# A linear-attention block with a one-token gated FFN beside it: dummy matmuls around the second tile's transposes, and a later place for two matmul batches and the down rows

## The chip, the cores and the metric

The kernel runs on one core of one Trainium2 chip. The metric is the device time of one execution in microseconds (us). The profiler also gives a span, from the first to the last instruction; of the same execution the time is about 1.7 us longer than the span. Lower is better.

## The reference, cut to what matters

Two blocks read the same `x` (2048 tokens of 1024) and are mixed by a sigmoid gate:

```python
def _A_ref(x, wqkv, wo):                    # linear attention, 32 heads of 32
    q, k, v = split(x @ wqkv)
    phi = lambda t: jnp.where(t > 0, t + 1, jnp.exp(t)) + 1e-6
    pq, pk = phi(q), phi(k)
    kv = einsum("bhsd,bhse->bhde", pk, v);  z = pk.sum(tokens)
    return (pq @ kv / (pq @ z + 1e-6)) @ wo
def _B_ref(x, w_r, w_gate, w_up, w_down):   # ONE token, the one with the largest x @ w_r
    y = (silu(x_sel @ w_gate) * (x_sel @ w_up)) @ w_down      # F = 3584
    return x with sigmoid(r_sel) * y added to that token's row
g = sigmoid((x * gate_w).sum(-1))
return g * a + (1 - g) * b
```

Block A is 16 tiles of 128 tokens times large matrices and fills TensorE. Block B is a single row times three 7 MB matrices: little arithmetic, much weight traffic. The kernel hides B under A.

## The kernel before: the parts that matter

A dummy is a matmul whose result nobody uses; it only keeps TensorE busy. `N_WARM` dummies and three short ones already stand at the start. The schedule of block B is set by tables that say after which unit of tile `t` a piece goes:

```python
N_WARM = 6
GU_AFTER = {(7, "end"): 4, (8, "end"): 4, (10, 3): 8, (12, 1): 8}   # batches of gate/up matmuls
FLUSH_AFTER = {(9, 2), (13, 0)}                                     # hps: turn h, so the down rows can begin
DOWN_STEPS = {10: (1, 1, 1, 1, 1, 1), 11: (1, 1, 1, 1, 1), 12: (1, 0, 1, 1, 1),
              13: (1, 1, 1, 1, 1), 14: (1, 1, 1, 1, 1), 15: (1, 1, 1)}
FFN_DEPTH = 9                                                       # weight buffers
```

The product with `w_down` isn't done on TensorE. VectorE does it in 28 rows, each a 128 x 1024 multiply-add into one accumulator, two rows to a weight tile:

```python
def compute(wt, kk, i2=i2, k0=k0, dk=dk):                 # one down row
    w, h1 = wt[:, 1024 * kk : 1024 * kk + 1024], hcol[:, ...]
    if i2 == 0 and kk == 0:
        dve.tensor_scalar(yacc, w, h1, None, op0=ALU.mult)
    else:
        dve.scalar_tensor_tensor(yacc, w, h1, yacc, op0=ALU.mult, op1=ALU.add)
```

(The accumulator `yacc` shares its memory with the gate sums, so the profile calls it `gacc`.) The same engine takes TensorE's results of the main stream out of PSUM, the memory that TensorE writes to. I call that an eviction: one of 128 x 512 for each key unit (`pk`) and each query unit (`pq_all`); value units are copied out by ScalarE. Key, value and query units share four PSUM buffers (`ps_work`, `bufs=4`).

Weight tiles of B are loaded in the order of `ffn_pieces`, and a load can go only when one of the nine buffers is free:

```python
yield from islice(g0, 6)          # gate tiles that VectorE sums (gacc)
...
for n in (2, 4):                  # 2 down tiles, 8 gate tiles, 4 down tiles, 8 up tiles, 8 down tiles
    yield from islice(dn, n)
    yield from islice(gu, 8)
yield from dn
yield from wo_pieces()
```

The main loop, cut:

```python
for t in range(4, NT):
    for nb in range(4):
        unit_KV(t, nb)                            # 8 matmuls of 512 columns; nb 0,1 key, 2,3 value
        if nb == 1 and t > 4 and t % 4 == 0:
            for t0 in range(t - 4, t):
                unit_KVACC(t0)                    # the kv block
        ffn_step(GU_AFTER.get((t, nb), 0))
        if (t, nb) in FLUSH_AFTER:
            ffn_flush()
        ...
        down_step(steps[nb])
    for i in range(Q_PER_T[t]):
        unit_Q(*q_units.popleft())
        ...
    ffn_step(GU_AFTER.get((t, "end"), 0))
    if t == 8:
        gate_reduce()                             # fp32 sums over partitions (gps), then silu, then h
```

After the loop, `down_finish` sums the 28 rows' accumulator over partitions (`yps`).

## Time and profile before

| before | |
|---|---|
| time, median of the first three runs | 251.35 us (250.92 to 251.53) |
| span of the profiled execution | 251.4 us |
| TensorE busy | 97% |
| VectorE busy | 65% |
| rise of the TensorE clock in that execution | 10.05 us |

Read it as a kernel that TensorE bounds almost everywhere. Time can only be gained where TensorE's stream has a hole or runs at half clock. The lines that carry this are in the prediction below.

### The profile page before, as it was taken

The numbers are of one execution on the slowest core, as the hardware profiler recorded it, in microseconds if no ns is written. First come the engines' busy times: TensorE is split into PE (matmuls) and PEld (weight loads), VectorE is DVE, ScalarE is ACT, GpSimd is POOL, SyncE is SP. The second block draws the span as 40 slices with busy tenths as digits, with TensorE's granted clock in tenths as the row PEclk, the third lists the DMA queues.
The fourth block names the chain that finished last, engine by engine and source line by source line (L and its number), as shares of the span: only waits on it lengthen the run. The fifth ranks groups of instructions, "written<-read, shape, count | busy, mean of one in ns | idle before, by whom it ended". The sixth has DMA issues, their size and how long they took to land.

```text
span 251.4 us, 4171 instructions
## 1 busy us (share of the span) xinstructions
PE 244.6 (97%) x1576; PEld 112.0 (45%) x1602; DVE 163.3 (65%) x257; ACT 125.7 (50%) x200; POOL 51.8 (21%) x102
## 2 busy tenths in 40 slices
PE   8999999999999999999999999999999999999994
PEld 3444445444444534444544444444444444444442
DVE  0036005244999469699699993585888999953442
ACT  2068334455455355545535644568888633333210
POOL 5000002010000100000033000210666689950000
PEclk9999999999999999999999999999999999999999
DMA  6999990008999992489699996130000564454122
GB/s 191 308 344 215 258 341 18 0 5 269 356 348 287 331 288 68 146 297 328 215 310 314 429 349 146 52 132 7 4 0 0 158 220 146 152 183 139 71 83 83
DMA packets 47242, 47.73 MB, mean 190 GB/s; under 512 B 18732, under 2 KB 35380, under 8 KB 47160
## 3 DMA queue, kind: packets, MB, share of 16 engines
q1 hardware_dynamic: 46552, 46.29, 60.2%
q0 software_dynamic: 640, 1.19, 1.6%
q8 instruction: 12, 0.20, 0.3%
q14 instruction: 6, 0.05, 0.1%
q10 hardware_dynamic: 32, 0.00, 0.0%
HBM read 39.34 MB, written 8.40 MB: 190 GB/s over the span
## 4 chain that ended last, share of the span: by engine, by line
PE 95%; DMA 2%; issue 1%; SPq 0%; DVE 0%; DVEq 0%
PE ps L80 87%; PE first L80 3%; DMA xnat<-in_A_x_dram 2%; PE kvacc L80 2%; PE dps L80 1%; PE rps L80 1%; PE pm L80 1%; PE pst L80 0%; PE gps L80 0%; SPq L80 0%; DVE ot L80 0%; PE yps L80 0%; PE xs_ps L80 0%; DVEq L747 0%; PE pt L80 0%
## 5 line engine op out<-in xcount | busy, mean ns | idle before, releaser
L80 PE MATMUL ps<-wkv,xT 128*128 128x512 bf16 x468 | 105.6, 379 | 0.6
L80 PEld LDWEIGHTS <-xT 128*128 128x128 bf16 x512 | 49.9, 99 | 60.9 <-issue 3.0
L80 PE MATMUL ps<-xT,wq 128*128 128x512 bf16 x248 | 57.5, 379 | 0.7 <-issue 0.5
L80 PE MATMUL ps<-m_sb,pq_all 128*128 128x512 bf16 (+2 forms) x259 | 55.3, 372 | 0.3
L80 ACT ACTIVATE u<-ps 128x512 f32<-128x512 f32 x60 | 35.8, 597 | 36.8 <-PE ps L80 36.1
L80 ACT ACTIVATE e<-u 128x512 f32<-128x512 f32 x64 | 40.3, 630 | 2.0
L650 POOL TENSOR_TENSOR pq_all<-pq_all,rb 128x512 bf16<-128x512 bf16 x32 | 36.6, 1172 | 14.4 <-DVE rb L80 14.0
L80 PEld LDWEIGHTS <-pq_all 128*128 128x128 bf16 x264 | 25.5, 98 | 30.2 <-issue 0.4
L80 PEld LDWEIGHTS <-wq 128*128 128x128 bf16 x256 | 24.3, 98 | 30.2 <-issue 2.1
L80 DVE SCALAR_TENSOR_TENSOR pq_all<-ps,e 128x512 bf16<-128x512 f32 x32 | 21.9, 686 | 23.8 <-ACT e L80 23.7
L80 DVE SCALAR_TENSOR_TENSOR gacc<-wt,hcol,gacc 128x1024 f32<-128x1024 bf16 x27 | 34.6, 1282 | 3.8 <-DMA wt<-in_B_w_down_dram 3.3
L80 ACT CAST vt<-ps 128x512 bf16<-128x512 f32 x32 | 18.8, 587 | 31.6 <-PE ps L80 31.6
L80 DVE SCALAR_TENSOR_TENSOR ot<-ps,gate,xg 128x512 bf16<-128x512 f32 (+2 forms) x33 | 23.8, 733 | 15.0 <-PE ps L80 14.2
L80 ACT ACTIVATE xg<-xt,omg 128x1024 f32<-128x1024 bf16 x16 | 18.1, 1145 | 25.9 <-DVE ot L80 25.9
L80 DVE SCALAR_TENSOR_TENSOR pk<-ps,e 128x512 bf16<-128x512 f32 x28 | 19.1, 686 | 7.5 <-ACT e L80 7.5
L209 POOL MEMSET vt<- 128x16 bf16 x16 | 2.4, 199 | 103.2 <-PE kvacc L80 102.6
L80 DVE STREAM_SHUFFLE rb<-rdp 128x512 f32<-128x512 f32 x32 | 22.8, 746 | 0.0
L80 DVE SCALAR_TENSOR_TENSOR gacc<-wt,xs_f,gacc 128x1024 f32<-128x1024 bf16 x14 | 17.4, 1279 | 0.5 <-DMA wt<-in_B_w_gate_dram 0.5
L80 PE MATMUL first<-wkv,xT 128*128 128x512 bf16 x31 | 8.9, 443 | 0.1
L80 DVE SCALAR_TENSOR_TENSOR pk<-first,e 128x512 bf16<-128x512 f32 x4 | 2.8, 692 | 9.3 <-ACT e L80 9.3
L80 DVE CAST r_bf<-rps 128x512 bf16<-128x512 f32 x1 | 0.7, 693 | 12.5 <-PE rps L80 12.5
L80 DVE RECIPROCAL rd<-dn 128x512 f32<-128x512 f32 x2 | 6.7, 3338 | 0.0
(104 smaller groups left out, 89.3 us busy)
## 6 DMA issues: line engine op xcount, KB each, us to landing
wt<-in_B_w_down_dram SPq DMA_DIRECT2D x14, 512.0 KB, 5.5
wt<-in_B_w_gate_dram SPq DMA_DIRECT2D x8, 512.0 KB, 7.3
wt<-in_B_w_up_dram SPq DMA_DIRECT2D x8, 512.0 KB, 8.6
xt<-xp SPq DMA_DIRECT2D x16, 256.0 KB, 3.0
out_dram<-ot SPq DMA_DIRECT2D x15, 256.0 KB, 2.0
wt<-in_B_w_gate_dram SPq DMA_DIRECT2D x8, 384.0 KB, 6.9
wt<-in_B_w_up_dram SPq DMA_DIRECT2D x8, 384.0 KB, 7.6
wkv<-in_A_wqkv_dram SPq DMA_DIRECT2D x8, 256.0 KB, 5.2
```

Source lines behind the costliest of these rows:

```text
L80: inst = fn(*a, **k)
L209: nc.gpsimd.memset(vt_t[t][:, :, :, 64:65], 1.0)
L650: nc.gpsimd.tensor_tensor(sl, sl, rb[:], op=ALU.mult)
```

## The change

The intent has two parts. At the start, short dummy matmuls are to keep TensorE busy around the second tile's transposes, so that its clock comes up early. In the middle, the first batch of up matmuls goes right behind the kv block, which saves a switch between kinds of matmul. The last of those batches goes, with the fp32 gate sums, a unit later, and everything behind them moves along: `hps` and the down rows.

```diff
-GU_AFTER = {(7, "end"): 4, (8, "end"): 4, (10, 3): 8, (12, 1): 8}
-FLUSH_AFTER = {(9, 2), (13, 0)}
+GU_AFTER = {(8, 1): 4, (9, 1): 4, (10, 3): 8, (12, 1): 8}
+FLUSH_AFTER = {(10, 1), (13, 0)}
-DOWN_STEPS = {10: (1, 1, 1, 1, 1, 1), 11: (1, 1, 1, 1, 1), 12: (1, 0, 1, 1, 1), 13: (1, 1, 1, 1, 1), 14: (1, 1, 1, 1, 1), 15: (1, 1, 1)}
+DOWN_STEPS = {10: (0, 1, 1, 1, 1, 1), 11: (1, 1, 1, 1, 1), 12: (0, 0, 1, 1, 1), 13: (1, 1, 1, 1, 1), 14: (1, 1, 1, 1, 2), 15: (1, 1, 1, 1)}
@@ start
-    wps = ps_ffn.tile([P, 16], BF, tag="f")
-    pe.transpose(wps[:], wrg_rows[:], ident[0:16, 0:16])
-    dve.tensor_copy(wrg_pad[:, :, 0:2], wps[:].rearrange(...))
+    pe.matmul(warm_ps[:, 0:16], lhsT=wrg_rows[:], rhs=ident[0:16, 0:16], start=True, stop=True)
+    dve.tensor_copy(wrg_pad[:, :, 0:2], warm_ps[:, 0:16].rearrange(...))
+    warm(4, 128, 128)
     unit_T(1)
+    warm(2, 128, 128)
@@ ffn_pieces
-        for n in (2, 4):
+        for n in (1, 4):
@@ main loop
+            if (t, nb) == (9, 1):
+                gate_reduce()
...
-        if t == 8:
-            gate_reduce()
```

(`warm` also gets an argument for the columns it writes; that is cut here.)

More of the change, by code (lines that the diff above doesn't have):

```diff
@@ L245, with warm @@
     warm_x = nc.const_aps.tensor(1.0, (P, 512), BF)
-    def warm(n, w=512):
+    def warm(n, w=512, o=0):
         for _ in range(n):
-            pe.matmul(warm_ps[:, 0:w], lhsT=warm_w, rhs=warm_x[:, 0:w], start=True, stop=True)
+            pe.matmul(warm_ps[:, o : o + w], lhsT=warm_w, rhs=warm_x[:, 0:w], start=True, stop=True)
     warm(N_WARM)
@@ L263 @@
     first_mm(0, 0, 1)
-    wps = ps_ffn.tile([P, 16], BF, tag="f")
-    pe.transpose(wps[:], wrg_rows[:], ident[0:16, 0:16])
-    dve.tensor_copy(wrg_pad[:, :, 0:2], wps[:].rearrange("p (w c) -> p c w", w=2))
+    pe.matmul(warm_ps[:, 0:16], lhsT=wrg_rows[:], rhs=ident[0:16, 0:16], start=True, stop=True)
+    dve.tensor_copy(wrg_pad[:, :, 0:2], warm_ps[:, 0:16].rearrange("p (w c) -> p c w", w=2))
+    warm(4, 128, 128)
     unit_T(1)
+    warm(2, 128, 128)
     for c in range(1, KC):
```

## The prediction

> **What bounds the kernel now.** I read the page's first part and its chain of waits first, to see which engine sets the end:
>
> ```profile
> span 251.4 us, 4171 instructions
> PE 244.6 (97%) x1576; PEld 112.0 (45%) x1602; DVE 163.3 (65%) x257; ACT 125.7 (50%) x200; POOL 51.8 (21%) x102
> ...
> PE 95%; DMA 2%; issue 1%; SPq 0%; DVE 0%; DVEq 0%
> ```
>
> TensorE (PE) is 97% busy and is 95% of the chain that ends last. VectorE (DVE) at 65% is the next. So a change can pay only by taking time out of the PE stream: a wait in it, a slow clock under it, or a price for switching between kinds of matmul. I looked for each in turn.
>
> The chain in order of time has one real wait, at the start (columns: start us, us, what):
>
> ```profile
> 1.91 4.73 DMA xnat<-in_A_x_dram
> 6.64 0.04 issue
> 6.68 1.03 PE pst L80 x8
> 7.72 5.75 PE first L80 x21
> ```
>
> The second 128-row tile of x lands at 6.64 us, its eight transposes (pst) follow, then the first matmuls. After that it is PE all the way to the last output. Next, the timeline of weight loads (PEld) in the opening stretch; each load precedes one matmul, so the distance between starts is the matmul step:
>
> ```profile
> 8.37 0.15 PEld L80 LDWEIGHTS <-xT 128*128 128x128 bf16 x1 [0.28 <-issue]
> 8.79 0.15 PEld L80 LDWEIGHTS <-xT 128*128 128x128 bf16 x1 [0.28 <-issue]
> 9.22 0.15 PEld L80 LDWEIGHTS <-xT 128*128 128x128 bf16 x1 [0.28 <-issue]
> 9.64 0.15 PEld L80 LDWEIGHTS <-xT 128*128 128x128 bf16 x1 [0.28 <-issue]
> 10.06 7.87 PEld L80 LDWEIGHTS <-xT 128*128 128x128 bf16 x37 [0.27 <-issue]
> ```
>
> Until 10.06 a 512-wide matmul takes a step of 0.427 us, afterwards 7.87/37 = 0.213 (0.216 from the starts of single matmuls). The trace's clock record has the rise at 10.05 us; the PEclk row prints 9 from the start and doesn't show it. Six useful matmuls run at half speed, from 7.51 to 10.05.
>
> In the PE timeline of the same stretch the hole before the second tile's transposes is visible:
>
> ```profile
> 4.94 1.06 PE L80 MATMUL first<-wkv,xT 128*128 128x512 bf16 x2
> 5.94 0.19 PE L80 MATMUL wps<-ident,wrg_rows 16*128 16x16 bf16 x1
> 6.68 1.03 PE L80 MATMUL pst<-ident,xnat 128*128 128x128 bf16 x8 [0.56 <-DMA xnat<-in_A_x_dram]
> ```
>
> For the middle part I read the PE and DVE timelines around the up batches (ps<-wt,xs_pad), the kv block (kvacc) and the fp32 gate sums (gps):
>
> ```profile
> 77.54 1.05 PE L80 MATMUL ps<-wt,xs_pad 128*32 128x512 bf16 x16
> 78.52 3.63 PE L80 MATMUL ps<-wkv,xT 128*128 128x512 bf16 x15
> 82.08 1.21 PE L80 MATMUL kvacc<-vt,pk 128*64 128x65 bf16 x64
> 83.22 3.63 PE L80 MATMUL ps<-wkv,xT 128*128 128x512 bf16 x15
> ...
> 96.58 0.68 DVE L80 TENSOR_TENSOR h_bf<-ps,sg 128x512 bf16<-128x512 f32 x1
> 97.32 0.25 PE L80 MATMUL hps<-sel,h_bf 128*128 128x4 bf16 x4
> ```
>
> The up batch streams four rounds of 512 columns side by side: 4 x 0.216 = 0.86 us. It occupies 78.52 - 77.54 = 0.98, so leaving it costs about 0.10; single starts give 0.094 into it and 0.096 out, and 0.093 and 0.099 for kvacc. These are the only holes in the stream there (a matmul record is missing every 50 or so, which looks like a hole of one step and is none). The hps matmuls begin 0.06 us after the DVE finishes h_bf at 97.26, and 0.278 after the matmul before them instead of 0.216: a wait of 0.06.
>
> **What the Trainium skill says.** "TensorE: Matmul & The Clock Gate", section "Part 1: The HAM clock gate": the PE starts at half clock and is released after a sufficiently busy window of 4096 cycles at 1.2 GHz (3.413 us); the window runs free, not from the kernel's start. The trace agrees on 0.427 against 0.216, and on the window: the clock record rises at 10.05 and falls 242.346 us later, 71.0 windows. So in this execution windows ended near 3.22, 6.64 and 10.05 us. The one ending at 6.64 holds the first tile's transposes and the hole, and did not release the clock.
>
> Same page, "Part 4: PE-mode transpose": transposes don't count as PE-busy in the same way. No trace here isolates that, but it explains why someone would set real matmuls on both sides of the transposes.
>
> "TensorEngine Tiling (Array Packing)", section "Key Properties": "Changing tiling mode (not just tile) drains the TensorE". The trace agrees: the 0.094 to 0.099 us above. It also shows the size of a switch between two tiled shapes: later on, kvacc to a 32-column batch, 0.126 between starts against about 0.03 of streaming, again 0.096.
>
> **The change part by part.** (a) Start. Four dummies of 128 columns go ahead of the second tile's transposes, two behind; the small router-row transpose becomes an ordinary matmul into the dummies' own bank, at the same place and size. At the slow clock a 128-wide matmul steps by 0.427/4 = 0.107 us, so 0.43 and 0.21. The instruction order of the built kernel adds a catch: the first of the four waits for the DVE copy out of that bank (wrg_pad), and the copy runs from 6.24 to 6.41. With 0.06 for the release, as at hps, they run from about 6.47 to 6.90, while the tile lands at 6.64. So with a slow clock the transposes slip by 0.22, and the two dummies behind add 0.21: 0.43 us of slow-clock work. If the clock still rises at 10.05, that work displaces one matmul (0.43/0.427) across the rise, where it costs 0.216: +0.22 us at the end.
> If instead the clock had risen at 6.64, the transposes would take 8 x 0.054 = 0.43 and the dummies 0.11, done by 7.22; the next weight block lands at 7.33 (trace's landing record), and 30 matmuls x 0.2158 from 7.38 end at 13.85 instead of 15.24: -1.39 us. The later weight blocks (7.97 to 11.38) arrive ahead of their use even then, and x for tiles 2 and 3 lands by 13.22.
> If the clock is up already before 6.6, as other window phases allow, old and new both wait for the landings at 6.64 and 7.33, and the dummies cost nothing: 0.
>
> (b) Middle. Moving the first up batch right behind kvacc replaces out-of-kvacc plus into-up (0.099 + 0.094) by one switch (0.096): -0.10 us. Moving the second up batch with the gate sums from the end of t=8 to after the second unit of t=9 leaves them adjacent: no switch gained. But the VectorE chain behind them (0.43 + 3.35 + 0.68 + 0.68 us) now has no pk result in between, since the units that follow are copied out by ScalarE, and hps comes 5 units (5 x 1.73 = 8.6 us) after the sums instead of 7. The 0.06 wait goes: -0.06. Sum of (b): -0.16 us.
>
> (c) The down rows start a unit later: the same 28, with two more of 1.28 us in the last two tiles of x. The DVE was idle 4.5 us ahead of 158.44 there, and the final row can end by about 155.5, before the sums over it at 158.18: 0. The copy of x into the scratch tensor is issued perhaps 5 us later, from 129 to 134, lands near 158 instead of 152.6, and is first needed by the row scatter at 160.28: 0.
>
> **Rivals.** First, the clock is rescued: the dummies lift the window ending at 6.64 over its threshold in every execution: -1.39 - 0.16, 249.8 us. Against it: they can start only at 6.47, so they fill 0.17 of that window. For it: the kernel's author put them there, and at other phases the window holds all of them.
> Second, the clock stays as late as in this profile and the dummies only delay: +0.22 - 0.16, 251.4 us. For it: the wait on the copy. Against it: the phase is free.
> Third, which I hold likeliest for most timed runs, the clock is mostly up before 6.6 already: a window of 3.413 that ends between about 3.5 and 6.0 contains nearly only real matmuls (2.5 of 3.4 us or more). The timed runs (250.92 to 251.53) are 1.7 us shorter than the profiled execution timed the same way (253.06); the profiler may cost that, but an early clock would also give 1.39. Then only (b) is left: 251.2 us.
> Fourth, the later schedule turns into a wait (a down tile's load, yps, wo): +0.5 to +1. The DMA slices have slack and DVE idles 4.5 us, so about 7%.
>
> **Range and chances.** Weights: third 55%, second 20%, first 18%, fourth 7%: 0.55 x 251.2 + 0.20 x 251.4 + 0.18 x 249.8 + 0.07 x 252 = 251.0. The three runs before spread over 0.6 us, so 8 in 10: 249.9 to 251.6. 2% is 5.0 us, and no path above reaches it: faster 0.01, same 0.985, slower 0.005.
>
> **What would show it.** The clock's rise in the weight-load steps: at 6.6 or before for the rescue, near 10 with pst at 6.9 for the delay. The first dummy starting 0.06 after the wrg_pad copy. kvacc directly followed by ps<-wt, with no 0.1 between full-width matmuls and it. hps 0.216 after its predecessor. A new wait ahead of yps, hps or ps<-wt, or a median beyond 1 us either way without a moved clock rise, would make the reasoning wrong.

## The result, and the profile after

| | median us | lowest to highest | runs |
|---|---|---|---|
| before | 251.27 | 250.92 to 251.53 | 4 |
| after | 253.45 | 253.08 to 253.68 | 4 |

The ratio is 1.0086, with a 95% interval from 1.0069 to 1.0104. A ratio here is the mean time of one kernel's runs over that of the other's runs of the same rounds; it leaves out the first run of each, so it isn't quite the ratio of the medians. Within 2%, and yet a clear loss of some 2.2 us, outside the predicted range (249.9 to 251.6).

First the page of the changed kernel: its span, and the last line of its chain by engine.

```profile
span 251.4 us, 4185 instructions
...
PE 74%; DVE 17%; DMA 4%; issue 2%; ACT 0%; DVEq 0%
```

Two things are to be seen. VectorE (DVE) has 17% of the chain that ends last, where it had 0%. And the span is 251.4 us, exactly that of the kernel before, although the time is 2.2 us longer. The second is an accident of the first profile. Of 55 executions of the kernel before that were run beside the experiments, 52 have spans from 249.1 to 249.9, two have 250.1 and 250.4, and one has 251.4; the profiled one was such a rare execution, with a late rise of the clock (10.05 us). So the whole span can't be compared between these two profiles. What can be is the stretch after the start, where the clock is up in both.

The start of the changed kernel, weight loads (start us, length, what, and in brackets the idle time before and what ended it):

```profile
6.28 0.45 PEld L80 LDWEIGHTS <-xnat 128*128 128x128 bf16 x8 [0.20 <-DMA xnat<-in_A_x_dram]
```

Eight transposes in 0.45 us are 0.056 each, the fast clock; its rise is at 4.02 us. TensorE still waits for the tile.

The middle, TensorE's timeline around the kv block:

```profile
79.14 1.21 PE L80 MATMUL kvacc<-vt,pk 128*64 128x65 bf16 x64
80.28 1.05 PE L80 MATMUL ps<-wt,xs_pad 128*32 128x512 bf16 x16
81.26 3.63 PE L80 MATMUL ps<-wkv,xT 128*128 128x512 bf16 x15
```

The up batch stands where it was meant to stand. To compare times free of the start, count from the first ordinary unit after it (the first `ps<-wkv` matmul: 15.24 before, 13.39 after). The gate batch that comes third begins 90.92 us later before (106.16) and 90.74 after (104.13): -0.18. So far the change pays as predicted. But the last matmul of the second sum of denominators (`dps`) comes 180.38 us after that first unit before, and 182.25 after: +1.87. I call this distance **the middle**; between 104 and 195 us, 2.05 us go. The view of waits (us in total, times, longest) shows where, first of before (which has no line of TensorE for VectorE), then of after:

```profile
DVE gacc L80 <- DMA wt<-in_B_w_down_dram: 3.3, 2, 1.8
```

```profile
DVE gacc L80 <- DMA wt<-in_B_w_down_dram: 6.2, 2, 3.1
PE ps L80 <- DVE pq_all L80: 0.9, 2, 0.5
```

VectorE waits 2.9 us longer for down tiles (in five other profiles without a loss this wait is 3.4 to 4.7 us, so the difference varies), and there is a wait of TensorE for VectorE that wasn't there. The queue that issues the loads explains the first. Before (start us, time the issues took, what, how many), then after:

```profile
81.83 18.63 SPq L381 DMA_DIRECT2D wt<-in_B_w_gate_dram  x8
103.04 4.91 SPq L464 DMA_DIRECT2D wt<-in_B_w_down_dram  x4
```

```profile
81.63 12.29 SPq L382 DMA_DIRECT2D wt<-in_B_w_gate_dram  x8
103.16 2.76 SPq L465 DMA_DIRECT2D wt<-in_B_w_down_dram  x4
...
122.92 5.76 SPq L465 DMA_DIRECT2D wt<-in_B_w_down_dram  x9
```

Eight gate tiles and one down tile fill all nine buffers. The next down tile is issued when the last row of the one in the buffers is done: at 103.04 before, where two down tiles stood ahead of the gate tiles, so four rows were done; at 103.16 after, where one stood ahead, so only two were done. The same happens again behind the eight up tiles (122.92). Each time VectorE runs out of rows and waits for a landing.

VectorE's timeline, the rows of interest, before and then after:

```profile
106.32 2.60 DVE L80 SCALAR_TENSOR_TENSOR gacc<-wt,hcol,gacc 128x1024 f32<-128x1024 bf16 x2 [1.52 <-DMA wt<-in_B_w_down_dram]
...
125.35 1.28 DVE L80 SCALAR_TENSOR_TENSOR gacc<-wt,hcol,gacc 128x1024 f32<-128x1024 bf16 x1 [1.77 <-DMA wt<-in_B_w_down_dram]
...
151.36 0.68 DVE L80 SCALAR_TENSOR_TENSOR pq_all<-ps,e 128x512 bf16<-128x512 f32 x1
...
158.44 0.69 DVE L80 SCALAR_TENSOR_TENSOR pq_all<-ps,e 128x512 bf16<-128x512 f32 x1 [4.49 <-ACT e L80]
```

```profile
106.86 1.28 DVE L80 SCALAR_TENSOR_TENSOR gacc<-wt,hcol,gacc 128x1024 f32<-128x1024 bf16 x1 [3.13 <-DMA wt<-in_B_w_down_dram]
...
127.13 1.29 DVE L80 SCALAR_TENSOR_TENSOR gacc<-wt,hcol,gacc 128x1024 f32<-128x1024 bf16 x1 [3.03 <-DMA wt<-in_B_w_down_dram]
...
147.56 5.24 DVE L80 SCALAR_TENSOR_TENSOR gacc<-wt,hcol,gacc 128x1024 f32<-128x1024 bf16 x4
152.71 0.69 DVE L80 SCALAR_TENSOR_TENSOR pq_all<-ps,e 128x512 bf16<-128x512 f32 x1
...
158.46 0.69 DVE L80 SCALAR_TENSOR_TENSOR pq_all<-ps,e 128x512 bf16<-128x512 f32 x1 [2.67 <-ACT e L80]
```

Read this as a race between two engines. Counted from the first unit, the rows go on after the second wait at 110.11 before (125.35 - 15.24) and at 113.74 after (127.13 - 13.39): VectorE is 3.63 us further behind TensorE. From there on it has no gap over 0.04 us until 155.8. The evictions of `pq_all` that lie among the rows, one for each tile of x here, I call grouped. Between the last two of them, at 143.37 and 152.71, lie 9.34 us of VectorE work: six rows, two `pk`, one `pq_all`. TensorE needs for one tile of x (four key and value units and a query unit, 40 matmuls) 40 x 0.2158 = 8.63 us. So VectorE doesn't catch up: it loses 0.7 us a tile, here as in the kernel before, where the same work also takes 9.34 us (142.02 to 151.36) but started early enough. The eviction stands behind four rows (5.24 us) while TensorE's result waits in PSUM. TensorE's own timeline shows the bill, before and then after:

```profile
111.04 7.07 PE L80 MATMUL ps<-wkv,xT 128*128 128x512 bf16 x32
...
148.31 7.07 PE L80 MATMUL ps<-wkv,xT 128*128 128x512 bf16 x32
```

```profile
109.01 7.28 PE L80 MATMUL ps<-wkv,xT 128*128 128x512 bf16 x32
...
144.11 1.89 PE L80 MATMUL ps<-wkv,xT 128*128 128x512 bf16 x8 [0.42 <-DVE pq_all L80]
...
153.45 1.89 PE L80 MATMUL ps<-wkv,xT 128*128 128x512 bf16 x8 [0.48 <-DVE pq_all L80]
```

The distances between single matmul starts, which also count the shorter holes, give 1.87 us of stalls between 134 and 155 us. In the kernel before they give none. The rest of the 2.05 is an earlier one: the 32 matmuls from 109.01 take 7.28 us, not 7.07. One step in them, until 112.67, is 0.21 us too long, right after an eviction of `pq_all` that VectorE ends at 112.62.

### The profile page after: what moved, and what is told of

Its sections match the earlier page's. It is cut to its first block, busy times and chain, and to the rows that moved or that the text cites. A ratio compares the mean times of both kernels' runs of the same rounds, so it can differ in the third digit from the quotient of the medians.

```text
span 251.4 us, 4185 instructions
## 1 busy us (share of the span) xinstructions
PE 243.6 (97%) x1583; PEld 111.3 (44%) x1608; DVE 163.2 (65%) x257; ACT 125.7 (50%) x200; POOL 51.8 (21%) x102
## 4 chain that ended last, share of the span: by engine, by line
PE 74%; DVE 17%; DMA 4%; issue 2%; ACT 0%; DVEq 0%
PE ps L80 67%; DVE gacc L80 13%; DMA wt<-in_B_w_down_dram 3%; PE first L80 3%; PE kvacc L80 1%; DMA xnat<-in_A_x_dram 1%; DVE eg L80 1%; DVE pk L80 1%; DVE pq_all L80 1%; PE dps L80 1%; PE rps L80 1%; PE pm L80 1%; PE pst L80 0%; PE gps L80 0%; ACT e L80 0%
## 5 line engine op out<-in xcount | busy, mean ns | idle before, releaser
L80 PE MATMUL first<-wkv,xT 128*128 128x512 bf16 x31 | 7.2, 379 | 0.2
L491 POOL DMA_DIRECT2D wt<-in_A_wo_dram x8 | 4.3, 538 | 14.2 <-DVE gacc L80 7.7
```

What stands on the lines that cost most here:

```text
L80: inst = fn(*a, **k)
L491: ld = eng.dma_start(out=wt[32 * r : 32 * r + 32, :].rearrange("p (c n) -> p c n", c=2), in_=wo_v[k // 2, r][:, 2 * (k % 2) : 2 * (k % 2) ...
```

## The experiments

The ratios are against the kernel before in the same rounds. The middle is from the one profiled execution of each.

**The dummies alone.** The kernel before with only the start of the change.

```diff
+    warm(4, 128, 128)
     unit_T(1)
+    warm(2, 128, 128)
```

> The kernel before with only the dummy matmuls (and the router rows as an ordinary matmul into their bank). Theory R (the 2.2 us come from the down rows waiting for their weights, the clock is up early in most timed runs): 0, within 0.3 us of before. Rival D (the dummies delay the start, the gain in the profiled execution was only its luckier clock window): +0.2 to +0.5 us. Rival C (the dummies rescue the clock in every run): -1.4 us.

Measured 251.46 us against 251.18: 1.001 (0.9998 to 1.0023). Middle 180.38, unchanged. The clock rose at 3.77 in the profiled execution, where the first matmuls then waited 0.78 us for the next weight block. The same again in a later round:

> The dummies alone once more, to be taken together with the first run (+0.1%, interval from 0 to 0.2%). If they cost nothing: within 0.15 us. If they cost: +0.25 us again.

251.35 against 251.18: 1.0000 (0.9985 to 1.0016), clock rise 4.1, middle 180.38. The dummies neither cost nor bring anything that shows. Whether they prevent the rare late start of the clock, 11 executions can't tell.

**The schedule alone.** The changed kernel without the new dummies.

```diff
-    warm(4, 128, 128)
     unit_T(1)
-    warm(2, 128, 128)
```

> The changed kernel without the dummy matmuls. Theory R: +2.0 to +2.4 us against before, as the whole change. Rival D: +1.7 to +2.0. In the trace two waits of the vector engine for a down tile of about 3 us each (near 103 and 123 us) and then TensorE stalls of about 1.9 us in sum between 134 and 154 us.

253.27 against 251.18: 1.0076 (1.006 to 1.0092). The whole loss is in the schedule. This profiled execution waits 7.2 us for down tiles, and its middle is 183.24, +2.86.

**Both moves, the old rows.** The batches and gate sums as changed, but `hps` a unit earlier, the old row table and two down tiles ahead.

```diff
-FLUSH_AFTER = {(10, 1), (13, 0)}
+FLUSH_AFTER = {(10, 0), (13, 0)}
-DOWN_STEPS = <changed>
+DOWN_STEPS = <before>
-        for n in (1, 4):
+        for n in (2, 4):
```

> Both moves of the up batches and gate sums and the dummies as in the changed kernel, but the second h transpose one unit earlier (after the first unit of t=10), with the old order of tiles (two down tiles ahead of the eight gate tiles) and the old row steps. Theory R: the 3 us wait near 103 shrinks to at most 1.5, no TensorE stalls after 130, so -0.16 us against before (-0.4 to +0.2). Rival M (the moved batches themselves cost, by pushing the vector engine's long reciprocal and the gate sums later): +1.5 us or more.

252.35: 1.0054 (1.0038 to 1.007). The first row starts 3.36 us later than before, counted from the first unit (5.08 in the changed kernel). The profiled execution was one of the two with the shortest span (250.2; the others up to 251.5) and lost only 0.28 in the middle. About half of the loss (1.17 us in the medians) stays with the old table, which neither expectation had (at most +0.2, or at least +1.5).

**A tenth buffer.** The changed kernel with ten weight buffers; the room comes from letting dead tiles be used again.

```diff
-FFN_DEPTH = 9
+FFN_DEPTH = 10
+    r_bf, rg_f, brow = h_bf[0], sg_t[0], h_bf[0][:, 0:256]    # in place of tiles of their own
```

> The changed kernel with ten weight buffers in place of nine (room made by letting three dead tiles be reused). Theory R (a down tile is fetched only when the buffer of the row before it is free): the second down tile is fetched with the gate tiles, both 3 us waits shrink under 1 us, TensorE stalls after 130 us go, so -0.2 to +0.3 us against before. Rival L (the rows simply start too late and two more of them lie in the last two tiles, whether or not their weights wait): +1.3 us or more remains.

252.29: 1.0063 (1.0036 to 1.009). The wait for down tiles falls from 6.2 us in two to 4.3 in three, the middle to 181.67 (+1.29). Weights that come earlier win back a part; they don't undo the loss (+1.1 us, between the two expectations). The rows still start 5.08 us late.

**Half of each row.** The changed kernel with rows of 512 columns (wrong; the comparison still passes, since one token's row weighs little in it).

```diff
-dve.scalar_tensor_tensor(yacc, w, h1, yacc, op0=ALU.mult, op1=ALU.add)
+dve.scalar_tensor_tensor(yacc[:, 0:512], w[:, 0:512], h1, yacc[:, 0:512], op0=ALU.mult, op1=ALU.add)
```

> The changed kernel with each of the 27 accumulating down rows over half the columns (0.69 us instead of 1.28 on the vector engine; the result is wrong on purpose; loads and all else unchanged). Theory V (from 127 to 153 us the vector engine, with rows begun 5 us later and two waits of 3 us for weights, is what bounds): no TensorE stall after 130 us, -0.3 to +0.2 us against before. Rival T (the moved batches cost on TensorE itself, or the later transfers do): +1.5 us or more remains.

Six runs from 251.57 to 255.44 us, ratio 1.0083 (1.004 to 1.0126). The slowest counts as slow (over 1.5% above the fastest); the ratio contains it and leaves out the fastest, which came first, and without the slow one it is 1.0064. The profiled execution, the fastest, has almost no stall: middle 180.36, one step 0.17 us too long at 143.28, with 8.8 us of waits for down tiles in three. Two other fast ones have spans of 251.9 and 252.7. Without the row work the loss can vanish, but the engine then catches up with its loads and waits for them. As a test of the row work it is inconclusive.

**The rows alone.** The kernel before with only the new row table and one down tile ahead; the batches and `hps` stay.

```diff
-DOWN_STEPS = <before>
+DOWN_STEPS = <changed>
-        for n in (2, 4):
+        for n in (1, 4):
```

> The kernel before with only the new row steps and the new order of tiles (one down tile ahead of the eight gate tiles); the up batches, gate sums, first h transpose and start as before. Theory V: rows begin 2 to 4 us later instead of 5 and both waits for weights grow to about 3 us, so +0.5 to +1.5 us. If the late start alone counts: +0.3 or less. If the order of tiles alone counts: +2.0 as the whole change.

252.14 against 251.46: 1.0024 (1.0008 to 1.0039); middle 181.02, +0.64. The one stall is in the last grouped eviction (waits):

```profile
PE ps L80 <- DVE pq_all L80: 0.5, 1, 0.5
```

So the table and the load order together take a third of what the change loses in its profile, although the first row starts at the same place.

**The first up batch alone.**

```diff
-GU_AFTER = {(7, "end"): 4, (8, "end"): 4, (10, 3): 8, (12, 1): 8}
+GU_AFTER = {(8, 1): 4, (8, "end"): 4, (10, 3): 8, (12, 1): 8}
```

> The kernel before with only the first up batch moved right behind the kv block. One switch of tiling less: -0.10 us in the trace between the end of the first matmuls and the second kv block; the rows start as before, so no TensorE stall. Timed: -0.3 to +0.1 us. Rival: the later release of four buffers delays the weight stream and the rows: +0.5 us or more.

251.24 against 251.46: 0.9994 (0.9979 to 1.0009). The middle is 180.27, 0.105 shorter, which is the switch that the prediction counted (0.10). In the times it can't be told from nothing.

**No dummies at all.** The kernel before without its own nine.

```diff
-    warm(N_WARM)
-    warm(3, 128)
```

> The kernel before without any dummy matmul. Measures what the clock at the start is worth. The clock rises only after the real matmuls have filled a window, at 8 to 13 us instead of about 4, so 6 to 15 of the first matmuls take a step of 0.427 us: +1.0 to +3.0 us, with a wider spread over the executions[...]. If the dummies do nothing: 0.

252.75 against 251.46: 1.0054 (1.0024 to 1.0084); the clock rises at 9.1 us in the profile. The old dummies earn about 1.3 us (0.6 to 2.1). The six new ones stand from 5.87 to about 7.0 us in the changed kernel's trace. In the seven profiles that keep the old start the rise is at 3.93, 3.97, 5.21, 5.79, 6.13, 6.61 and 10.05 us, so in four of them the clock is up before that.

**The gate exponential moved late, in four kernels.** The loads of the gate logits queue behind the down tiles, and the small gate computation stands ahead of the last query units. I moved it behind them, on four kernels, to see whether it held part of the loss.

```diff
     down_finish()
-    gates()
...
     strict[0] = False                 # behind the remaining query units
+    gates()
```

On half rows:

> The half-width rows once more (result wrong on purpose), with the gate exponential taken behind the last Q unit instead of ahead of the last two. In the run without this its profiled execution had no stall (middle as fast as before), yet three of six executions were 2 to 4 us longer. Theory G (the gate logits' load, queued behind the copy of x, landed at 156.1 us and was asked for at 156.7; where it comes later, ScalarE[...] holds back the evictions and TensorE stalls): all executions within 1 us of each other and -0.3 to +0.2 us against before. Rival S (the spread comes from elsewhere, a start with a late clock): half of them stay 2 to 4 us longer.

254.21: 1.0136 (1.0096 to 1.0177), all six executions between 253.74 and 256.83, so neither expectation held. On the changed kernel:

> The changed kernel with the gate exponential behind the last Q unit. Theory V (the vector engine's rows are its bound between 127 and 153 us): +1.7 to +2.2 us against before, nearly all of the loss stays, since the loads landed 2.2 us ahead of their use there. If the gate load were the main cause: under +0.5.

254.37: 1.012 (1.0092 to 1.0149). On both moves with the old rows:

> Both moves with the old rows and order and the earlier h transpose (it measured +1.2 us, its profiled execution showed +0.3), with the gate exponential behind the last Q unit. Theory G: the difference between the two was the gate load, so +0.2 to +0.6 us remains. Rival S: +1.0 or more.

252.79: 1.0056 (1.003 to 1.0081). On the first up batch alone:

> The candidate to beat both: the kernel before with the first up batch right behind the kv block and the gate exponential behind the last Q unit. One tiling switch less and one load off the path: -0.1 us, -0.4 to +0.2 timed.

252.34: 1.0037 (1.0012 to 1.0062). None gained. The edit itself opens a wait at 202 to 204 us in all four profiles, this line of the last one's waits for instance:

```profile
PE ps L80 <- DVE ot L80: 0.7, 1, 0.7
```

This wait makes the times of little use as a test, but not the middle, which ends ahead of it: 182.25 on the changed kernel and 180.27 on the first up batch, as without the edit. So this theory fell. The half-row profile, whose middle is 182.19, shows one way in which that kernel loses time: TensorE waits 1.84 us until 144.87 for an eviction that stands behind two rows whose weights landed at 142.58.

**Six rows left out.** The changed kernel without 6 of the 28 rows (wrong).

```diff
-                else:
+                elif not (kk == 1 and 6 <= i2 <= 11):
                     dve.scalar_tensor_tensor(yacc, w, h1, yacc, op0=ALU.mult, op1=ALU.add)
```

> The changed kernel with six of its 28 down rows not computed (the second row of tiles 6 to 11, behind the last wait for weights; result wrong on purpose; every load stays). It frees 7.7 us of the vector engine after 127 us. Theory V (from there on the row work queued ahead of the PSUM evictions is the bound): no TensorE stall after 130 us in the profile, -0.3 to +0.4 us against before. Rival (weights that land late, or anything else): +1.0 us or more remains.

252.74 against 251.18: 1.007 (1.0022 to 1.0119), and again of two kinds: spans of 249.9, 250.1 and 250.4, and of 251.9, 253.1 and 253.7. The profiled one is of the second kind. VectorE's timeline:

```profile
142.04 2.61 DVE L80 SCALAR_TENSOR_TENSOR gacc<-wt,hcol,gacc 128x1024 f32<-128x1024 bf16 x2 [2.29 <-DMA wt<-in_B_w_down_dram]
144.56 0.68 DVE L80 SCALAR_TENSOR_TENSOR pq_all<-ps,e 128x512 bf16<-128x512 f32 x1
```

A third wait for weights, with the eviction behind it in the engine's order: TensorE then waits 1.75 us, until 145.30. In three of six executions less row work leaves only 0.4 to 0.8 us of the loss (251.58 to 251.97 against 251.18); the profiled one shows that a late tile does the same harm as late work. The other two slow ones have no trace.

**The late start alone.** The kernel before, batches and load order untouched, with `hps` and the first rows later.

```diff
-FLUSH_AFTER = {(9, 2), (13, 0)}
+FLUSH_AFTER = {(10, 1), (13, 0)}
-DOWN_STEPS = {10: (1, 1, 1, 1, 1, 1), ...
+DOWN_STEPS = {10: (0, 2, 1, 1, 1, 1), ...
```

> The kernel before with the first h transpose three units later (after the second unit of t=10) and the first two rows then done together; old order of tiles, batches where they were. The late start alone: the rows begin about 5 us later. If the late start is the larger part of the loss: +0.8 to +1.8 us, with TensorE stalls after 130 us. If the order of the tiles is: under +0.4.

254.05 against 251.18: 1.0106 (1.0088 to 1.0125); middle +2.58. Its waits:

```profile
PE ps L80 <- DMA wt<-in_B_w_gate_dram: 1.4, 1, 1.4
PE ps L80 <- DVE pq_all L80: 0.9, 2, 0.5
```

Starting the rows late is enough for a loss of this size, more than was expected (+0.8 to +1.8), but only half of it comes the same way: the steps of the matmuls give 1.3 us of waits for evictions. The first line is the other half, a price of the old load order: with two down tiles ahead, the eighth gate tile gets its buffer only when late rows have freed it, and TensorE waits 1.4 us for it. That may be why the change puts one down tile ahead instead of two, which, together with the new table, costs something itself (the rows alone, above).

**The changed kernel again.**

> The changed kernel again, in the same rounds: +1.9 to +2.4 us, and in its profile an early clock, two waits of the vector engine for a down tile of about 3 us and TensorE stalls of about 1.9 us after 130 us.

253.41 against 251.18: 1.0092 (1.0075 to 1.0109); middle 182.44 (+2.06), 6.4 us of waits for down tiles. The loss repeats.

**A PSUM buffer for the late query units.** If four shared buffers are the limit, a query result in a bank of its own frees one of them.

```diff
-        ps = ps_work.tile([P, 512], F32, tag="w")
+        ps = ps_red.tile([P, 512], F32, tag="gps") if own else ps_work.tile([P, 512], F32, tag="w")
...
-            unit_Q(*q_units.popleft())
+            unit_Q(*q_units.popleft(), own=t >= 11)
```

> The changed kernel with the Q results of t=11 to 14 in the PSUM bank that the gate sums no longer need, so that a late eviction of Q holds none of the four work banks. Order of all engines and all loads unchanged. Theory V (the stall is the bank held by a Q eviction queued behind rows): the TensorE waits on pq_all near 144 and 153 us go, at least 1.2 of the 1.9 us in the middle come back, +0.2 to +1.0 us against before. Rival W (the weights or the vector engine's total work bound the stage): the stalls move to the pk evictions and +1.8 us or more remains.

253.59 against 251.16: 1.0094 (1.0078 to 1.011); middle 182.22, +1.84. The waits:

```profile
PE ps L80 <- DVE pk L80: 1.6, 1, 1.6
...
PE ps L80 <- DVE pq_all L80: 0.2, 1, 0.2
```

The two waits for `pq_all` are nearly gone, and one for `pk` of 1.6 us has taken their place; the sum is the same. That is what the rival expected. So in this place one more buffer decides only where TensorE stops. That it stops is decided by when VectorE gets through its queue.

**The kernel before again, one look.**

> The kernel before, one more profile. If the late rise of the clock in its first profile (10.05 us, span 251.4) was a rare start: a rise before 7 us and a span of 249.1 to 249.9 us, middle unchanged at 180.4 us from the first tile-2 matmul to the last den matmul. If it is the rule in profiled executions: a rise near 10 and 251 us.

Span 249.8 us, time 251.51, clock rise 6.61, middle 180.37. The start, weight loads:

```profile
7.25 6.79 PEld L80 LDWEIGHTS <-xT 128*128 128x128 bf16 x32 [0.47 <-issue]
```

From 7.25 on a step takes 0.212 us; in the first profile it was 0.427 until 10.06. The middle agrees to 0.01 us. So the first profile's start was the exception and its middle was not.

**What the runs say together.** Take the start of the last grouped `pq_all` eviction (151.36 before, 152.71 after), counted from the first unit of each trace, and set it beside the change of the middle:

| kernel | last grouped eviction starts, us after the first unit | middle against 180.38 |
|---|---|---|
| before, before again, both runs of dummies alone | 136.10 to 136.12 | 0 |
| both moves, old rows | 137.80 | +0.28 |
| both moves, old rows, gates late | 137.91 | +0.40 |
| rows alone | 138.16 | +0.64 |
| tenth buffer | 138.81 | +1.29 |
| after; after with gates late | 139.32 | +1.87 |
| after again | 139.50 | +2.06 |
| late start alone | 140.09 | +2.58 |
| schedule alone | 140.32 | +2.86 |

In the nine traces with a loss, the first number less the second is between 137.44 and 137.52. VectorE may be 1.4 us later at this place than it was (137.5 - 136.1); every microsecond after that is a microsecond of the middle. Two traces don't fit, half rows with late gates (136.38, +1.81) and six rows left out (136.72, +2.15): TensorE stalled there at the grouped eviction before. Counted the same way it starts at 130.69 and 130.97, in the kernel before at 126.78; less the loss that is 128.88 and 128.82, a slack of 2.1 us. That is 0.7 more than the slack one tile later, and 0.7 is what VectorE loses in a tile (9.34 - 8.63). The table says that the end of this stretch follows VectorE; what made VectorE late differs from kernel to kernel.

The 2.2 us in the times and the 1.87 and 2.06 in the two profiles are of a kind. The loss varies between executions, and the schedule alone, profiled once, lost 2.86.

No version beat both kernels. The first up batch alone is better than the changed kernel, and isn't told apart from the kernel before.

## Why the prediction was wrong

**(a) The start: right.** It gave three outcomes and held "the clock is up already" for the likeliest. Two runs of the dummies alone at 1.001 and 1.0000 bear this out, and so does the rise before 6.6 us in five of the seven profiles with the old start. In the second profile of the kernel before it came at 6.61, late in the second tile's transposes (6.01 to 6.72) and not ahead of them. The first dummy does wait for the copy to `wrg_pad`, 0.34 us in the trace, but with the clock up that ends before the tile lands. The guess that the 1.7 us between timed and profiled execution might be an early clock was right as well: with the rise at 6.61, the profiled time is 251.51.

**(b) The middle: right in mechanism and size.** -0.16 predicted, -0.18 in the trace as far as the third batch; -0.10 for the first batch, -0.105 by itself. `hps` has no wait left: it starts 0.216 us after the matmul before it, as predicted.

**(c) The down rows: this step failed.** It took the rows to start "a unit later", 1.73 us; they start 5.08 us later, since they can't begin before `hps`, which starts 82.08 us after the first unit before and 87.09 after. And the prediction put 0 on the delay: "The DVE was idle 4.5 us ahead of 158.44 there, and the final row can end by about 155.5, before the sums over it at 158.18: 0." Its endpoint is right: the final row ended at 154.59 and the sums began at 158.20. Its fault was to take the sums over the accumulator for the only thing that waits for the rows. The same engine empties PSUM in program order, so the rows are also ahead of `pq_all` and `pk`, and TensorE feels the delay there, well before the idle time that was to absorb it. The idle time ahead of the eviction at 158.46 is still 2.67 us long in the changed trace, unused. (The copy of x, which it put at perhaps 134 us, was issued at 128.74 and landed at 154.20; it cost nothing.)

The slack was therefore mis-sized. It is 1.4 us at the last grouped eviction, not 4.5 at the end. And the delay was not only two rows: with the late start the two waits for weights grow by 2.9, and after them VectorE goes on 3.63 us behind its old place. At the eviction it is 3.20 behind (139.32 - 136.12); 3.20 - 1.4 = 1.8, against 1.87 measured.

**The rivals.** The fourth, "the later schedule turns into a wait (a down tile's load, yps, wo)", is the nearest to what happened and named the down tiles. It got 7% and +0.5 to +1. The runs show about +2, and the wait that TensorE has is not for the load: the load makes VectorE late, and VectorE makes TensorE late. The step there, "The DMA slices have slack", was read off an average. A tile that can't be issued before a buffer frees isn't helped by free bandwidth.

**The signs.** The prediction named "a new wait ahead of yps, hps or ps<-wt" as its refutation. The new wait is ahead of `ps<-wkv`, the most ordinary units of all, where it didn't look. Its other sign, a median over 1 us away without a moved clock rise, did come as far as the times show (+2.2); where the clock rose in the timed runs isn't seen.

**What stays open.** How much of the loss is row work that starts late and how much is weights that land late isn't split cleanly. Where work was taken away, waits for weights came in its place (8.8 and 8.4 us in two profiles) and half of the executions stayed slow; a tenth buffer changed both at once. No run moved the batch with the gate sums alone, or the start of the rows under the new load order alone. Nor is it shown what makes those two kernels fall into two kinds of execution.

The page "Perfetto Trace Analysis" of the Trainium skill says in its section "Optimization Strategy" that the most-contended engine can change over time within a kernel. This agrees, with numbers: VectorE is 65% busy over the whole and has no gap between 127.13 and 155.8 us. The prediction judged VectorE by its one idle stretch of 4.5 us, not by this one.

## What to carry to other kernels

When side work on an in-order engine is moved, look for every instruction that stands behind it in that engine's order, above all those that empty PSUM, and measure the slack at the first of them, not at the end of the side work. Where the last piece of a load order has just enough buffers, a later start of its reader also makes the next load later, so the delay grows on its way. Compare stretches between fixed points of two traces before comparing spans: a rare start of one profile hid 2 us here.

## What the Trainium skill lacked or had wrong

- "TensorEngine Tiling (Array Packing)", section "Key Properties", names the drain on a change of mode and gives no size. Here it is 0.093 to 0.099 us a switch in the trace, and taking one out shortened the middle by 0.105 us.
- "TensorE: Matmul & The Clock Gate", section "Part 4: PE-mode transpose", says that the full clock doesn't engage for transposes. In the changed kernel's trace, with the clock up since 4.02 us, eight 128 x 128 transposes take 0.45 us, 0.056 each, half of the 0.107 that they take at the slow clock in the first profile of the kernel before.
- "Vector Engine (DVE) Microarchitecture Reference", section "5.2 Measured stream behaviour on trn2 (trn3 not measured)", gives 1.0417 ns a column and about 75 ns an instruction, from which one estimates 1.14 us for 1024 columns; it doesn't treat a multiply-add with bf16 weights into an fp32 accumulator. Here the 128 x 1024 down row took 1.28 us, and four in a row, each of which reads the sum of the one before, 5.24. In such a chain whole rows start 1.32 us apart and half rows 0.787, so a column costs 1.04 ns, as the page says, and a row some 0.25 us besides.
- "TensorE: Matmul & The Clock Gate", section "Part 1: The HAM clock gate", says that the number of slow matmuls differs from run to run, but neither it nor another page says how often a late start comes. Here the rise of the clock lies between 3.77 and 10.05 us in the profiled executions, and the late one goes with a span of 251.4 us where 52 of 55 executions have 249.1 to 249.9.
